# Carried turns sent from SyncE's queue, and the two functions of the sign made on ScalarE for the first group too

## The chip, the core and the metric

The kernel runs on one core of one Trainium2 chip. The metric is the device time of one launch in microseconds (us); where several launches are given, their median. The core has TensorE (PE in the profile, its weight loads PEld), VectorE (DVE), ScalarE (ACT), GpSimd (POOL) and SyncE (SP, which here only issues transfers). ScalarE can issue transfers from its queue as well.

## What is computed

A gated linear recurrence with complex gates, then a feed-forward layer of three maxed projections. Cut to what matters:

```python
q, k, v, a_re, a_im            # each (4, 8, 768, 48): batch, heads, steps, head_dim, float32
mag = sqrt(a_re**2 + a_im**2); scale = minimum(mag, 0.999) / (mag + 1e-6)
a = (a_re + 1j * a_im) * scale
for t in range(768):
    S = a[:, :, t, :, None] * S + k[:, :, t, :, None] * v[:, :, t, None, :]   # complex state, 48 x 48
    y[:, :, t] = einsum('bhd,bhde->bhe', q[:, :, t], S.real)
x = y.transpose(0, 2, 1, 3).reshape(3072, 384)
h = maximum(maximum(x @ w1, x @ w2), x @ w3)      # 384 -> 768
out = h @ w_out                                   # 768 -> 384
```

The four weights come as 64-bit floats, and the kernel rounds them to 32 bits itself, in twelve blocks.

## The kernel before

**Groups and tiles.** The 768 steps are cut into six stretches of 128; two batches go together. That makes 12 groups (g), each of two tiles x = 2g and 2g + 1 (c = 0, 1), one per batch, with 8 heads x 48 = 384 columns each. Within a tile the recurrence is done as small matmuls on blocks.

**From the gates to the rotated k and q.** `gate_steps` (lines 343 to 393) turns a group's a_re and a_im (`ar`, `ai`) into a log magnitude (`Ln`, line 369) and the tangent of half the angle (`w`, line 381). Line 383 takes the sign of `ar`. Two functions of this sign then go into `ai` and `ar`: (1 - sign)/4 at line 385 or 388, and -sign/pi at line 386 or 389. Groups after the first make them on ScalarE, the first group (g = 0, done in two halves of 128x384) on GpSimd. Line 391 takes the carried turn of the group before off the first row of `ai`, on GpSimd. `turns` (lines 395 to 424) takes the arctangent (ScalarE, another activation table, loaded at line 133), multiplies by `ar` (line 401), adds `ai` (line 402), and sums along the steps by matmuls (`cs`, line 410). ScalarE rounds the sum (`t`, line 413), VectorE takes the fraction (`nf`, line 415), and the last rows of `nf` are transferred into `carry` for the next group: four transfers of 0.8 KB per group (line 424), by ScalarE's queue. `sines` (lines 426 to 435) takes |nf| (`af`, line 430) and sine and cosine (`CS`, four activations by line 112). `products` multiplies k and q by magnitudes (line 475), by `CS` into `uk` and `uq` (line 480), and `uk` by `En` (line 485).

**From there to the output.** `turn` transposes uk and uq on TensorE (`tp`) and ScalarE copies them out (`K` line 497, `Q` line 501). `cut` makes decay factors (`F` on TensorE, `f` on ScalarE, line 112). `prep` multiplies by them on VectorE (line 528: Q, KB, QB, QG). `scores` makes A and B on TensorE, `gather` picks them into `atm` (line 576), `state` updates the state (`dk`, lines 624 to 627), `outputs` makes `y`, copied out as `xT` (line 652). The feed-forward part is `up` (three projections: line 668 copies, line 670 takes the maximum) and `op` (line 678 copies out, line 680 writes).

**Weights.** A block is loaded (line 304), and `weight_round` uses ScalarE (lines 330 and 320) and VectorE (lines 331, 333, 321, 322). All twelve blocks are rounded in about the first 105 us, in between the first two groups.

**Order.** The program is written in one order (a first group by hand, then `weave`, which merges steps by written-down fractions, then `group(g)`), and the framework's scheduler orders each engine's queue from it, except that TensorE's order is fixed by hand up to the second group (line 120), and activations that depend on the table keep their order (line 108). Each engine runs its queue strictly in order. PSUM holds four tiles of two banks for all matmul results, so a matmul can wait for a copy-out of an earlier tile. Transfers take turns over eight completion semaphores, whichever queue issues them, and an issue waits until the transfer before it on its semaphore has landed.

Of the kernel before, what the change touches and what calls it, by code (L numbers as in the profile page):

```python
# [16 lines left out]
AF = mybir.ActivationFunctionType  # L17
OP = mybir.AluOpType
# [33 lines left out]
def kernel(  # L52
# [13 lines left out]
    nc = tc.nc  # L66
# [18 lines left out]
    HC = DM // 2  # L85
# [16 lines left out]
    T = {}  # L102
# [8 lines left out]
    def act(**kw):  # L111
        tab(nc.scalar.activation(**kw))  # L112
# [14 lines left out]
    def banks(nm, n=None):  # L127

        ps = psum.tile([P, 2, 512], FP, tag="ps", name=nm)
        return ps if n is None else ps.rearrange("p a n -> p (a n)")[:, 0:n]  # L130
# [204 lines left out]
    def flat(t):  # L335
        return t.rearrange("p c h d -> p (c h d)")
# [6 lines left out]
    def gate_steps(g, cs):  # L343
        lo, hi = cs[0] * DM, (cs[-1] + 1) * DM

        def part(nm):
            t = T[nm, g]
            return (flat(t) if len(t.shape) == 4 else t)[:, lo:hi]

        def s0():  # L350
            if lo == 0:
                for nm in "Lwe":
                    T[nm, g] = nat1.tile([P, W], FP, tag=nm, name=nm)
                T["Ln", g] = nat2.tile([P, W], FP, tag="Ln", name="Ln")
            L, w, ar, ai = part("L"), part("w"), part("ar"), part("ai")
            nc.scalar.activation(out=w, in_=ar, func=AF.Square)
            nc.scalar.activation(out=L, in_=ai, func=AF.Square)

            nc.vector._custom_dve(dve_ops.TENSOR_ADD_SAT, out=L, in0=L, in1=w, s0=LARGE, s1=SMALL)
            act(out=L, in_=L, func=AF.Ln)  # L360

        def s1():

            L, w, e = part("L"), part("w"), part("e")
            act(out=w, in_=L, func=AF.Exp, scale=0.5)
            act(out=e, in_=L, func=AF.Exp, scale=-0.5)
            act(out=e, in_=e, func=AF.Ln, scale=1e-6, bias=1.0)
            nc.scalar.activation(out=L, in_=L, func=AF.Relu, scale=-0.5, bias=lnmax)
            nc.vector.scalar_tensor_tensor(out=part("Ln"), in0=L, scalar=-LNMAX, in1=e, op0=OP.add, op1=OP.add)  # L369

        def s2():

            L, w, e, ar, ai = part("L"), part("w"), part("e"), part("ar"), part("ai")
            nc.scalar.activation(out=e, in_=ar, func=AF.Abs)
            nc.vector.tensor_tensor(out=w, in0=w, in1=e, op=OP.add)
            act(out=L, in_=w, func=AF.Ln)
            act(out=L, in_=L, func=AF.Exp, scale=-1.0)

            (nc.gpsimd if g > 1 else nc.vector).tensor_tensor(out=ai, in0=ai, in1=L, op=OP.mult)  # L379
            nc.vector.tensor_tensor(out=w, in0=w, in1=L, op=OP.mult)  # L380
            nc.vector.scalar_tensor_tensor(out=w, in0=w, scalar=2.0, in1=ai, op0=OP.subtract, op1=OP.mult)

            nc.scalar.activation(out=ar, in_=ar, func=AF.Sign, bias=tiny)
            if g > 0:
                nc.scalar.activation(out=ai, in_=ar, func=AF.Copy, scale=-0.25, bias=0.25)  # L385
                nc.scalar.activation(out=ar, in_=ar, func=AF.Copy, scale=-1.0 / math.pi)
            else:
                nc.gpsimd.tensor_scalar(out=ai, in0=ar, scalar1=-0.25, scalar2=0.25, op0=OP.mult, op1=OP.add)
                nc.gpsimd.tensor_single_scalar(out=ar, in_=ar, scalar=-1.0 / math.pi, op=OP.mult)
            if g % NS > 0:  # L390
                nc.gpsimd.tensor_tensor(out=ai[0:1], in0=ai[0:1], in1=T["carry", g], op=OP.subtract)  # L391

        return [s0, s1, s2]

    def turns(g, cs, meanwhile):

        w, ar, ai = T["w", g], flat(T["ar", g]), flat(T["ai", g])
        for part in [[c] for c in cs] if g == 0 else [cs]:
            n = slice(part[0] * DM, (part[-1] + 1) * DM)
            act(out=w[:, n], in_=w[:, n], func=AF.Arctan)  # L400
            nc.vector.tensor_tensor(out=w[:, n], in0=w[:, n], in1=ar[:, n], op=OP.mult)
            nc.vector.tensor_tensor(out=w[:, n], in0=w[:, n], in1=ai[:, n], op=OP.add)  # L402
        meanwhile(2)
        for c in cs:
            ps = banks("cs", DM)

            for ch in range(2):
                for j in range(2):
                    at = c * DM + j * HC
                    mm(out=ps[j * L64:(j + 1) * L64, ch * HC:(ch + 1) * HC], lhsT=upto[:, ch * L64:(ch + 1) * L64],  # L410
                       rhs=w[:, at:at + HC], start=True, stop=True)
            t = nat2.tile([P, DM], FP, tag="t", name="t")
            nc.scalar.activation(out=t, in_=ps, func=AF.Copy, bias=MAGIC)
            nf = nat2.tile([P, DM], FP, tag="nf", name="nf")
            nc.vector.scalar_tensor_tensor(out=nf, in0=t, scalar=MAGIC, in1=ps, op0=OP.subtract, op1=OP.subtract)
            T["nf", g * C + c] = nf
            if g == 0:
                sines(g, [c])
            if (g + 1) % NS > 0:
                if c == 0:  # L420
                    T["carry", g + 1] = nat1.tile([1, W], FP, tag="carry", name="carry")
                for j in range(2):
                    last, at = (j + 1) * L64, c * DM + j * HC
                    nc.scalar.dma_start(out=T["carry", g + 1][:, at:at + HC], in_=nf[last - 1:last, HC:])

    def sines(g, cs):
        for c in cs:
            nf = T["nf", g * C + c]
            t = nat2.tile([P, DM], FP, tag="t", name="af")
            nc.scalar.activation(out=t, in_=nf, func=AF.Abs)  # L430
            CS = nat2.tile([P, H, 2, D], FP, tag="CS", name="CS")

            act(out=CS[:, :, 0], in_=hv(t), func=AF.Sin, scale=TWOPI, bias=hpi)
            act(out=CS[:, :, 1], in_=hv(nf), func=AF.Sin, scale=-TWOPI)
            T["CS", g * C + c] = CS

    def angles(g, cs, meanwhile=lambda n: None):

        table("trig_and_small")
        turns(g, cs, meanwhile)  # L440
        if g > 0:
            sines(g, cs)
        table("natural_log_exp_and_others")
# [434 lines left out]
```

## Time and profile before

| what | value |
|---|---|
| median of 10 launches | 679.93 us (678.76 to 681.74) |
| the profiled launch, its own time | 680.61 us |
| its span in the profile | 678.9 us |
| busy: PE, DVE, ACT, POOL | 604.5, 496.9, 388.3, 121.3 us |
| mean granted TensorE clock | 0.977 |
| carry transfers from ScalarE's queue | 40 issues, median 0.60 us each, 3.7 us from issue to landing |
| POOL, lines 388 and 389 | 2 + 2 instructions of 128x384: 1.04 and 0.51 us, 1.29 and 1.17 us |
| ACT, lines 385 and 386 (later groups) | 11 + 11 instructions of 128x768, 0.84 us each |

Times are read from one profiled launch, in microseconds from the start of its span. A bracket at the end of a timeline row tells how long the engine stood idle before the row and what ended that; "ACTq" or "SPq" rows are the queue's issue of transfers, which does not count as busy. Rows of a few instructions are merged (x4).

### The profile page before, as it was taken

How to read it: one execution, taken by the hardware profiler on the slowest of the kernel's cores; microseconds unless marked ns; L12 is line 12 of the kernel's file. 1: busy time of each engine (PE TensorE's matmuls, PEld its weight loads, DVE VectorE, ACT ScalarE, POOL GpSimd, SP SyncE). 2: the span in 40 equal slices, each digit the busy share in tenths (PEclk: the TensorE clock that was granted, in tenths of full speed). 3: DMA queues.
4: the chain of work that ended last, by engine and by line, in shares of the span. 5: the costliest groups of instructions: out<-in, count | busy, mean ns of one | idle time of the engine just before them, and what ended most of it. 6: DMA issues, size and time to landing. Idle time of an engine off the chain costs nothing.

```text
span 678.9 us, 24518 instructions
## 1 busy us (share of the span) xinstructions
PE 604.5 (89%) x10844; PEld 497.4 (73%) x10844; DVE 496.9 (73%) x662; ACT 388.3 (57%) x618; POOL 121.3 (18%) x130
## 2 busy tenths in 40 slices
PE   1134677889999999999999999999999999999997
PEld 0033665777878878878878878878878878887785
DVE  4798989986887887887786787788787878755111
ACT  6687776686386386557475565755754854430000
POOL 8500101403213113013013013023023023000000
PEclk9977987999999999999999999999999999999999
DMA  6684443331331331330330331320420220000000
GB/s 134 167 250 96 125 105 65 68 65 35 58 57 33 62 61 25 66 62 19 66 66 16 73 59 27 70 62 18 73 56 15 37 49 2 2 26 3 13 13 24
DMA packets 139050, 39.38 MB, mean 58 GB/s; under 512 B 131648, under 2 KB 134720, under 8 KB 138944
## 3 DMA queue, kind: packets, MB, share of 16 engines
q1 hardware_dynamic: 137664, 37.78, 25.7%
q8 instruction: 85, 1.39, 0.8%
q10 hardware_dynamic: 1280, 0.03, 0.1%
q14 instruction: 21, 0.17, 0.1%
HBM read 33.03 MB, written 4.72 MB: 56 GB/s over the span
## 4 chain that ended last, share of the span: by engine, by line
PE 66%; ACT 12%; DVE 9%; issue 7%; POOL 4%; DMA 1%; ACTq 0%; DVEq 0%; POOLq 0%
PE up L117 33%; PE op L117 13%; PE y L117 6%; PE tp L117 4%; PE B L117 3%; PE cs L117 2%; PE A L117 2%; ACT CS L112 2%; PE dk L117 2%; PE sums L117 1%; ACT e L112 1%; ACT K L497 1%; ACT L133 1%; DVE QB L528 1%; ACT f L112 1%
## 5 line engine op out<-in xcount | busy, mean ns | idle before, releaser
L117 PE MATMUL up<-xT,w 128*128 128x256 f32 (+1 forms) x1404 | 294.5, 367 | 5.2 <-ACT f L112 2.4
L117 PEld LDWEIGHTS up<-xT,w 128*128 128x128 f32 x1404 | 247.8, 191 | 41.9 <-ACT f L112 5.7
L117 PE MATMUL op<-wo,hT 128*128 128x384 f32 x288 | 99.1, 495 | 0.8 <-ACT K L497 0.4
L668 ACT COPY hT<-up 128x768 f32<-128x768 f32 (+2 forms) x27 | 19.6, 725 | 115.2 <-PE up L117 115.2
L117 PEld LDWEIGHTS op<-wo,hT 128*128 128x128 f32 x288 | 53.4, 191 | 35.4 <-ACT K L497 1.4
L670 DVE TENSOR_TENSOR hT<-hT,up 128x768 f32<-128x768 f32 (+2 forms) x54 | 46.3, 857 | 43.5 <-PE up L117 43.0
L379 POOL TENSOR_TENSOR ai<-ai,L 128x768 f32<-128x768 f32 x10 | 21.7, 2174 | 287.3 <-ACT L L112 138.7
L528 DVE TENSOR_TENSOR Q<-Q,f 112x512 f32<-112x512 f32 x48 | 40.5, 844 | 38.3 <-ACT f L112 38.3
L528 DVE TENSOR_TENSOR QB<-Q,f 112x512 f32<-112x512 f32 (+1 forms) x48 | 61.9, 1326 | 0.0
L117 PE MATMUL y<-atm,vb 128*32 128x64 f32 x1536 | 45.8, 227 | 3.1 <-DVE atm L576 2.9
L117 PEld LDWEIGHTS y<-atm,vb 128*32 128x32 f32 x1536 | 39.1, 114 | 12.6 <-issue 8.7
L117 PE MATMUL y<-QG,g 112*32 112x64 f32 x1408 | 44.5, 222 | 0.0
L112 ACT ACTIVATE f<-F 48x296 f32<-48x296 f32 x96 | 39.6, 413 | 0.8
L117 PEld LDWEIGHTS y<-QG,g 112*32 112x32 f32 x1408 | 38.1, 112 | 0.0
L475 POOL TENSOR_TENSOR k<-E,k 128x384 f32<-128x384 f32 x20 | 24.6, 1230 | 69.7 <-ACT E L112 69.7
L117 PE MATMUL B<-QB,KB 112*32 112x80 f32 x1536 | 33.8, 242 | 2.4 <-DVE QB L528 1.9
L485 DVE TENSOR_TENSOR uk<-uk,En 128x768 f32<-128x768 f32 x24 | 22.9, 954 | 17.4 <-PE tp L117 17.4
L117 PE MATMUL sums<-Ln,mid 64*64 64x192 f32 x192 | 14.9, 361 | 22.5 <-DVE Ln L369 22.5
L117 PE MATMUL cs<-w,upto 128*64 128x192 f32 x192 | 19.6, 349 | 17.3 <-DVE w L402 13.8
L391 POOL TENSOR_TENSOR ai<-ai,carry 1x768 f32<-1x768 f32 x10 | 19.2, 1918 | 84.8 <-ACT ai L385 81.4
L117 PE MATMUL tp<-ident,uk 128*112 128x128 f32 x192 | 27.6, 292 | 7.3 <-DVE uk L480 7.3
L576 DVE COPY_PREDICATED atm<-masko,B 128x256 f32<-128x256 uint8 x72 | 31.6, 439 | 3.2
(106 smaller groups left out, 997.9 us busy)
## 6 DMA issues: line engine op xcount, KB each, us to landing
ar<-in_a_re_dram SPq DMA_DIRECT2D x24, 192.0 KB, 3.9
ai<-in_a_im_dram SPq DMA_DIRECT2D x24, 192.0 KB, 3.6
k<-in_k_dram SPq DMA_DIRECT2D x96, 48.0 KB, 2.4
q<-in_q_dram SPq DMA_DIRECT2D x96, 48.0 KB, 2.4
vb<-in_v_dram SPq DMA_DIRECT2D x192, 24.0 KB, 2.2
out_dram<-ot SPq DMA_DIRECT2D x24, 192.0 KB, 2.2
raw<-in_moe_w_dram SPq DMA_DIRECT2D x5, 768.0 KB, 4.9
w<-in_moe_w_dram SPq DMA_DIRECT2D x2, 768.0 KB, 7.0
```

The source lines that it names most:

```text
L112: tab(nc.scalar.activation(**kw))
L117: ins = f(**kw)
L133: tab(nc.scalar.preload_act_table_set(nm))
L379: (nc.gpsimd if g > 1 else nc.vector).tensor_tensor(out=ai, in0=ai, in1=L, op=OP.mult)
L391: nc.gpsimd.tensor_tensor(out=ai[0:1], in0=ai[0:1], in1=T["carry", g], op=OP.subtract)
L475: eng.tensor_tensor(out=hd(T[nm, x]), in0=E, in1=hd(T[nm, x]), op=OP.mult)
L485: nc.vector.tensor_tensor(out=u, in0=u, in1=two(T["En", x]), op=OP.mult)
L497: nc.scalar.copy(out=T["K", x][0:DD], in_=src)
L528: nc.vector.tensor_tensor(out=out, in0=in_, in1=f.to_broadcast([DD, 2 * H - g, n, 8]), op=OP.mult)
L576: nc.vector.copy_predicated(out=out, mask=mask, data=data)
L668: nc.scalar.copy(out=dst, in_=ps)
L670: nc.vector.tensor_tensor(out=dst, in0=dst, in1=ps, op=OP.max)
```

## The change

For the first group the two functions of the sign are made by ScalarE like in all others, and the four carry transfers of each group are issued from SyncE's queue.

```diff
             nc.scalar.activation(out=ar, in_=ar, func=AF.Sign, bias=tiny)
-            if g > 0:
-                nc.scalar.activation(out=ai, in_=ar, func=AF.Copy, scale=-0.25, bias=0.25)
-                nc.scalar.activation(out=ar, in_=ar, func=AF.Copy, scale=-1.0 / math.pi)
-            else:
-                nc.gpsimd.tensor_scalar(out=ai, in0=ar, scalar1=-0.25, scalar2=0.25, op0=OP.mult, op1=OP.add)
-                nc.gpsimd.tensor_single_scalar(out=ar, in_=ar, scalar=-1.0 / math.pi, op=OP.mult)
+            nc.scalar.activation(out=ai, in_=ar, func=AF.Copy, scale=-0.25, bias=0.25)
+            nc.scalar.activation(out=ar, in_=ar, func=AF.Copy, scale=-1.0 / math.pi)
             if g % NS > 0:
                 nc.gpsimd.tensor_tensor(out=ai[0:1], in0=ai[0:1], in1=T["carry", g], op=OP.subtract)
...
-                    nc.scalar.dma_start(out=T["carry", g + 1][:, at:at + HC], in_=nf[last - 1:last, HC:])
+                    nc.sync.dma_start(out=T["carry", g + 1][:, at:at + HC], in_=nf[last - 1:last, HC:])
```

The scheduler orders the queues anew for the changed program. As built, TensorE's queue is the same. Around the change the others differ like this:

- ScalarE, first group: one Copy of each half's pair stands after each of the activations that follow it; the second half's pair lies between the last activations before the first table load. Further on, the second half's `t`, `af`, `CS` and the table load back now stand ahead of the first `K`; before they stood behind it.
- ScalarE, second group: `t`, `t`, one weight step (line 330), `af`, `af`, `CS`; the four carry issues between are gone. Later `K`, `Q`, `f` stand ahead of line 357 where line 357 stood ahead of `K`.
- VectorE: in the first group the first `k` product (line 475) stands ahead of line 381; in the second group the four line 480 products stand ahead of the weight steps of lines 321, 331 and 322, which stood ahead of them; in later groups they alternate with the three `atm` picks from B, which stood ahead of them.
- SyncE: the four carries stand right behind a group's loads of `ar` and `ai` and ahead of its loads of k and q. In the second group they stand between the first `ar` load and the other three of these loads, and the loads of v into the first buffer, which stood ahead of the k and q loads, stand behind them, with the two `ai` loads of the group after behind that.

## The prediction

> **What bounds the kernel now.** I read first the busy time of the engines by stage (columns: stretch, its length, busy time and instructions of PE, PEld, DVE, ACT and POOL, granted clock, share of the transfer engines, GB/s).
>
> ```profile
> 0.00:30.00 30.00, 3.16 (x34) 1.72 (x34) 16.25 (x42) 20.24 (x37) 25.09 (x70) 1.00 0.60 143
> 30.00:50.00 20.00, 8.52 (x141) 7.00 (x145) 18.65 (x27) 15.54 (x24) 0.00 (x0) 0.80 0.86 248
> 50.00:85.00 35.00, 20.59 (x376) 18.27 (x370) 32.37 (x50) 26.14 (x39) 2.04 (x1) 0.82 0.47 111
> 85.00:105.00 20.00, 13.33 (x320) 12.27 (x320) 17.96 (x30) 13.25 (x22) 0.00 (x0) 0.87 0.44 99
> 105.00:133.00 28.00, 23.02 (x548) 19.45 (x540) 26.85 (x31) 19.46 (x30) 9.85 (x6) 0.91 0.30 58
> 133.00:180.00 47.00, 43.49 (x917) 36.89 (x918) 38.11 (x52) 29.61 (x47) 10.29 (x6) 1.00 0.27 51
> 180.00:660.00 480.00, 477.49 (x8483) 391.31 (x8482) 344.84 (x435) 262.95 (x418) 73.99 (x47) 1.00 0.21 41
> ```
>
> From 180 us on TensorE is the bound: it is idle for 480.00 - 477.49 = 2.51 us of 480. Nothing that ScalarE, GpSimd or SyncE saves there is worth more than these 2.5 us, though eight of the ten carries lie there. Before that VectorE is the bound from 30 to 133 us (busy 93, 92, 90 and 96% of the four stretches), because it rounds the weights as well. So the change is worth what it takes out of the first 180 us, as far as VectorE's idle time lets it. Next I read the timelines of VectorE, GpSimd, ScalarE and TensorE there, at the two places that the change touches.
>
> ```profile
> 25.95 0.56 DVE L401 TENSOR_TENSOR w<-w,ar 128x384 f32<-128x384 f32 x1 [1.28 <-POOL maskf L144]
> 28.88 0.56 DVE L401 TENSOR_TENSOR w<-w,ar 128x384 f32<-128x384 f32 x1 [2.37 <-POOL ar L389]
> ...
> 27.08 0.51 POOL L388 TENSOR_SCALAR ai<-ar 128x384 f32<-128x384 f32 x1
> 27.67 1.17 POOL L389 TENSOR_SCALAR ar<-ar 128x384 f32<-128x384 f32 x1
> ...
> 23.02 1.00 ACT L112 ACTIVATE E<-sums 128x384 f32<-128x384 f32 x2 [2.36 <-DVE k L475]
> 24.03 1.28 ACT L133 ACT_TABLE_LOAD   x1
> 37.55 1.01 ACT L497 COPY K<-tp 112x1024 f32<-112x1024 f32 x1 [1.95 <-PE tp L117]
> 86.87 3.70 ACTq L424 DMA_DIRECT2D carry<-nf  x4
> 90.62 0.94 ACT L430 ACTIVATE af<-nf 128x384 f32<-128x384 f32 x2 [3.83 <-DVE ex L331]
> 93.61 1.93 PE L117 MATMUL tp<-ident,uk 128*112 128x128 f32 x8 [3.75 <-DVE uk L480]
> 104.29 0.66 PE L117 MATMUL y<-atm,vb 128*32 128x64 f32 x16 [2.92 <-DVE atm L576]
> ```
>
> Both edits are on the path there. GpSimd gets to the second half's sign functions at 27.08, after its masks, and VectorE stands still 2.37 us for them. ScalarE issues four carries for 3.70 us between `t` and `af`, with `nf` long done (VectorE's L415 pair ran from 86.26 to 87.38), and TensorE waits 3.75 us for what comes of `af`.
>
> **Part 1, the sign functions (0 to 30 us).** GpSimd loses 1.04 + 0.51 + 1.29 + 1.17 = 4.0 us. ScalarE gains four Copies of 128x384; no such row exists, the nearest is L374 of that form: 515 ns long, with the next one starting 0.41 to 0.42 us after it. So 4 x 0.42 = 1.7 us. The first pair falls into ScalarE's 2.36 us of idle time before 23.02. The second pair lies around the last E's, ahead of the table load. In the new order VectorE makes the first k product one instruction (L381, 0.6 us) earlier, and the GpSimd instructions that stretched its neighbours are gone (L379 0.85 against 0.56 in the first half): it starts at about 21.4, not 22.40. Then E at 21.9, Copy 22.5, E 22.95, Copy 23.35, table load 23.75 (before 24.03), arctangent 25.05, and line 401 runs at 25.7 and 26.15 instead of 25.95 and 28.88: 2.7 us won. If k comes no earlier, the second pair sets the table load back by 0.84 us to 24.87 and 1.6 us are won. I take 2.7.
>
> Here a rule of the Trainium skill speaks against the change: "ScalarE: Activation LUTs", in Rules for kernel authors, wants plain multiplies and adds on VectorE, not ScalarE, and budgets about 0.3 us + 0.83 ns per element for an activation. By it each Copy takes 0.3 + 384 x 0.00083 = 0.62 us (an estimate), the second pair costs 0.4 us more than above, and 2.3 us are won. The measured 0.42 us decides; VectorE, which the rule prefers, is the engine that waits.
>
> **Part 2, 30 to 85 us.** The first group's two carries a half are cheap on ScalarE (0.50 to 0.61 us each, mostly beside running activations), but the new order moves the second half's `t`, `af`, `CS` and the 1.28 us table load ahead of K, into the 1.95 us that ScalarE waited at 37.55. Replayed with the durations of the rows: nf at 29.4, uk (L480) at 32.1 (before 34.49), table load done at 35.2, transpose 33.1 to 35.05, K 35.2, the weight steps L330 and L320 0.8 each, Q 37.7, and the four f done at 40.25 where they ended at 45.5: 5.2 us earlier. VectorE cannot follow all of that; in its new order QB ends at 45.0 instead of 49.37, **4.4 us won**. Bounds: 2.7 if VectorE only shifts, 5.2 if it follows. The loads don't stop this: the raw weights were issued at 29.96 to 31.6 and landed 4.8 us later, and the first is wanted at 36.1. From 50 to 85 us VectorE is full in both (one wait of 1.67 us for L330 comes back as about 1.5), so 4.4 us arrive at the next `cs`, at 80.3 instead of 84.74.
>
> **Part 3, the carries of the second group (85 to 105 us).** On the new clock `t` ends at 82.3, L330 (0.8) stands before af at 83.1, the first CS pair is done at 84.85, and L480 starts at 84.9 where it started at 92.50. TensorE's tp comes 7.6 us earlier. But the weight steps that VectorE did meanwhile (0.87 + 0.47 + 0.87 = 2.2 us) now follow, and only VectorE's idle time can be won: 20.00 - 17.96 = 2.0 us, of which one new wait for L320 behind K, Q and two f gives back about 1. So y, after the last atm pick, gains 4.4 + 2.0 - 1.0 = 5.4. **I carry 5.5 us on.**
>
> Here a second rule: "DMA: Bandwidth & Descriptors", section Issuing engines are not separate DMA queues, says that issuing from several engines saves only the sequencer's time to initiate a transfer, usually small relative to the transfer. By it part 3 would be nothing and 4.4 us would be carried on. The row shows 3.70 us of issue in front of af, as long as a carry's 3.7 us to landing; so I keep the 1 us.
>
> **Part 4, 105 to 180 us.** To 133 us VectorE idles 1.15 us of 28: 0 more. K no longer stands behind L357 (0.85 us), which may take 0.4 us off TensorE's wait for f at 123.3; I take 0. From 133 to 180 TensorE idles 47.00 - 43.49 = 3.5 us (0.76 for uk, 0.94 for hT, 0.56 for K, 0.56 for f, the rest smaller). ScalarE gets 2.65 us back in front of af at 138.40, which serves all of these, but K now stands behind two more activations. I take 1.5 of 0 to 3.
>
> **Part 5, SyncE and the rest.** SyncE issues 40 x 0.60 = 24 us more. In a steady group it is free from 184.56 to 189.74, between its last `ai` issue and its first k load, and four carries take 2.4 us; nf is done at 184.0 and the k loads behind wait for uk later anyway. In the first group its loads stood still 6.0 us until 38.52 for a carry of ScalarE's on their semaphore; that goes. The carry is read (L391) a group later. VectorE's atm picks, now alternating with L480, end some 2.5 us later (190.2 for 187.7 at the steady group of 183 us), and y needs them at about 198. After 180 us I count 0 (bounds 0 and 1.5).
>
> **Sum.** 5.5 + 1.5 = 7.0 us, from the profiled launch's own 680.61: 673.6. The median of the runs lies 0.7 below that launch, so 679.93 - 7.0 = **672.9 us**.
>
> **Rivals.** *Half of it.* VectorE is at 90 to 96%: what TensorE and ScalarE win early is only work put off, part 2 keeps 2.7 and part 3 gives 1: 3.7, and little after; 676.2. For it: the full row of VectorE. Against: in part 2 it has 1.35 us idle plus a shorter stretch to fill.
>
> *Slower.* The loads of v that now stand ahead of the `ai` loads of g = 3. On the old clock k and q are issued until 106.8; two blocks of v follow, at 5.95 us each as at 107.49, or 9.26 as at 85.36; then the `ai` loads land (2.9 us) at about 123, at worst 129. ScalarE reaches L357 at 123.2. If they land later than that, ScalarE stands, and behind it are En, E, the table load and the arctangent, then L401 and cs on the path; it turns into a loss once it exceeds the 5.5 us, at about 128.7. With v, k and q all at the slower rate (12 us of k and q become 18), landing at 135 costs 11.8 - 5.5 = 6.3: 686. Against: k and q start 7 us earlier with uk.
>
> *No change.* Both edits only fill waits, VectorE is saturated from the first weight on, and the order costs as much as it gains: 679.9. Against: 2.37 us idle at 28.88 on the bounding engine.
>
> **Chances.** The forecast 0.62 (its own range 669.5 to 675.5), half 0.22, no change 0.05, slower 0.11. A difference of 0.2%, 1.36 us, is about the least that can be told from none. Faster: 0.62 + 0.22 = 0.84; within: 0.05; slower: 0.11. The range runs from 669.0, where the upper bounds of parts 2 and 4 and of the rest (0.8 + 1.5 + 1.5) are all but reached, to 677.5, which takes in the half case: 0.16 is left out above.
>
> **What would show it.** Right: line 401's second row near 26.2 with no GpSimd wait; QB done near 45; no ACTq rows, af within 1 us of `t` and L330; TensorE's wait at the second tp below 1 us; TensorE idle some 2.5 us of the last 480 before the tail. Wrong: a wait of ScalarE for `ai` at L357 near 117, SyncE still in v loads there, or VectorE waits for L330 or L320 of several us between 50 and 100.

## The result, and the profile after

Fourteen launches of the changed kernel have a median of 676.11 us (673.23 to 678.15), beside 679.58 us for 49 launches of the kernel before. The ratio is 0.9945, 95% interval 0.9932 to 0.9958: 3.7 us won (2.9 to 4.6), where 7.0 were forecast. The profiled launch took 676.42 us, its span is 674.7 us, its mean granted clock 0.972. From line 390 of before on, line numbers are four lower (397 is the arctangent's product, 411 `nf`, 471 the k product, 476 `uk`, 497 `Q`, 572 `atm`, 622 the state).

Busy time by stage, with the columns of the first view of the prediction:

```profile
0.00:30.00 30.00, 5.95 (x48) 3.40 (x48) 18.89 (x48) 22.93 (x44) 23.11 (x66) 1.00 0.60 144
30.00:50.00 20.00, 9.75 (x183) 8.65 (x184) 19.49 (x29) 14.61 (x22) 0.00 (x0) 0.73 0.90 255
50.00:85.00 35.00, 21.56 (x378) 18.55 (x381) 30.17 (x45) 26.31 (x40) 2.04 (x1) 0.74 0.45 122
133.00:180.00 47.00, 44.69 (x921) 37.48 (x915) 37.12 (x49) 29.89 (x49) 9.72 (x6) 1.00 0.23 43
180.00:660.00 480.00, 477.07 (x8389) 391.38 (x8378) 339.75 (x433) 261.49 (x414) 73.53 (x47) 1.00 0.20 41
```

GpSimd's four instructions at the start are gone, but its busy time fell only from 25.09 to 23.11 us, since its masks took 2.0 us longer. Behind 180 us TensorE idles 2.93 us, before 2.51: hardly anything changed there. But VectorE, which should have become fuller from 50 to 85 us, is emptier (30.17 against 32.37), and the clock is lower in two stages (0.73 for 0.80 and 0.74 for 0.82). Now the rows that answer to those shown of before (start, duration, engine, line, operation):

```profile
24.88 1.15 DVE L397 TENSOR_TENSOR w<-w,ar 128x384 f32<-128x384 f32 x2 [1.67 <-ACT w L112]
...
34.89 1.01 ACT L493 COPY K<-tp 112x1024 f32<-112x1024 f32 x1
...
54.06 0.56 DVE L331 TENSOR_SCALAR ex<-ex 128x768 f32<-128x768 f32 x1 [2.32 <-ACT ex L330]
57.28 0.96 DVE L321 CUSTOM_DVE_ANT_0 ex<-w,ex 128x1536 uint16<-128x1536 uint16 x1 [0.98 <-ACT w L320]
...
81.15 2.83 PE L117 MATMUL cs<-w,upto 128*64 128x192 f32 x16 [3.43 <-DVE w L398]
...
85.21 0.93 ACT L426 ACTIVATE af<-nf 128x384 f32<-128x384 f32 x2
...
88.87 1.08 PE L117 MATMUL tp<-ident,uk 128*112 128x128 f32 x8
...
100.45 0.57 PE L117 MATMUL y<-atm,vb 128*32 128x64 f32 x16 [4.50 <-DVE atm L572]
```

Of the kernel before, `cs` was not shown yet:

```profile
84.74 1.52 PE L117 MATMUL cs<-w,upto 128*64 128x192 f32 x16 [3.43 <-ACT ex L330]
```

Every wait that the change was to remove is gone: VectorE's 2.37 us for GpSimd, ScalarE's 1.95 us before K, its four carry issues before `af`, TensorE's 3.75 us before the second `tp`. Yet others have grown: VectorE's waits for L330 and L320, and TensorE's wait for the last pick before y (4.50 us for 2.92). And `cs` itself takes 2.83 us where it took 1.52.

When comparing the two launches a start-up difference has to come off. The first half's `Ln` (L369) ran at 12.20 us here and at 13.11 us before, ahead of everything that the change touches. The column of these two launches in the table has this 0.9 us taken off; that is the most it can be worth, since in a kernel whose GpSimd makes the sign functions an early start was partly lost (`e_carry`, below).

| gain at | forecast | changed against before, less 0.9 | the same pair with TensorE kept busy (below) |
|---|---|---|---|
| end of the arctangent's products | 2.7 | 2.5 | 2.7 |
| end of QB | 4.4 | 3.7 | 4.0 |
| second group's `cs` | 4.4 | 2.7 | 3.1 |
| `uk`, second group | 7.6 | 4.5 | 6.0 |
| y behind the last pick | 5.4 | 2.9 | 6.1 |
| `cs` of g = 2 | 5.5 | 2.2 | 5.5 |
| `cs` of g = 3 | 7.0 | 3.2 | 6.6 |
| span | 7.0 | 3.3 | 5.8 |

### The profile page after: what moved, and what is told of

Read it like the earlier page. It is cut to its first block, busy times and chain, and to the rows that moved or that the text cites. A ratio compares the mean times of both kernels' runs of the same rounds, so it can differ in the third digit from the quotient of the medians.

```text
span 674.7 us, 24524 instructions
## 1 busy us (share of the span) xinstructions
PE 607.2 (90%) x10844; PEld 498.7 (74%) x10844; DVE 490.0 (73%) x662; ACT 390.4 (58%) x622; POOL 119.1 (18%) x126
## 4 chain that ended last, share of the span: by engine, by line
PE 59%; ACT 14%; issue 5%; DVE 2%; DMA 0%; POOL 0%; POOLq 0%; ACTq 0%; DVEq 0%
PE up L117 29%; PE op L117 13%; PE y L117 6%; PE tp L117 2%; ACT CS L112 2%; ACT e L112 2%; PE B L117 2%; PE cs L117 2%; PE sums L117 2%; ACT L133 2%; PE dk L117 1%; PE A L117 1%; ACT K L493 1%; DVE Ln L369 1%; ACT ar L383 1%
## 5 line engine op out<-in xcount | busy, mean ns | idle before, releaser
L524 DVE TENSOR_TENSOR QB<-Q,f 112x512 f32<-112x512 f32 (+1 forms) x48 | 53.3, 1148 | 0.0
L117 PEld LDWEIGHTS y<-atm,vb 128*32 128x32 f32 x1536 | 39.2, 114 | 13.9 <-issue 10.6
L524 DVE TENSOR_TENSOR KB<-K,f 112x768 f32<-112x768 f32 x24 | 38.2, 1590 | 0.0
L357 ACT ACTIVATE L<-ai 128x768 f32<-128x768 f32 (+1 forms) x13 | 10.3, 793 | 40.0 <-DVE w L380 32.6
```

Source lines behind the costliest of these rows:

```text
L117: ins = f(**kw)
L524: nc.vector.tensor_tensor(out=out, in0=in_, in1=f.to_broadcast([DD, 2 * H - g, n, 8]), op=OP.mult)
```

## The experiments

**My theory** after the comparison: part 1 is right; part 2's new order gave nothing that lasted; parts 3 and 4 are worth 1 to 2 us, of which TensorE's half clock at `cs` hid some. Rivals: the sign edit is the whole gain; the new order is the whole gain; the half clock only covers waits for a full VectorE. Ratios below are to the kernel before on the same chip, with their 95% intervals; 0.001 is 0.68 us.

### Each edit alone

`e_sign` has only the first hunk of the diff, `e_carry` only the second.

> Only the sign edit; the carries stay on ScalarE's queue. As built, ScalarE's queue keeps the second half's af, CS and the table load behind the first K, so this run has part 1 without parts 2 and 3. Theory (the two edits add up, the sign edit gives the 2.6 us seen at the arctangent's product): 677.0, line 397's second row near 25.4, K near 35, but f still done some 8 us behind K as before. Rival A (the sign edit is the whole gain, the carries are worth nothing): 675.9, as fast as the changed kernel. Rival B (VectorE is full, an earlier start is only put off, and the new order is the whole gain): 679.4.

Measured 676.91 us, ratio 0.9955 (0.9936 to 0.9975). The product's rows run from 25.00 to 26.03, K at 34.15, f ends 8.0 us behind it. The theory's number; 675.9 lies in the interval too.

> Only the carry edit; the first group's two functions of the sign stay on GpSimd. As built, ScalarE's second half (t, af, CS, table load) stands ahead of the first K here too. Theory (edits add up): 678.2, about 1.3 us below the kernel before, line 401's second row still near 28.9, f done 1.5 to 2.5 us earlier than 45.5. Rival A (carries worth nothing): 679.6. Rival B (the order is the whole gain): 676.2.

Measured 678.61 us, 0.9985 (0.9966 to 1.0004); line 401's second row at 28.08, f done at 44.0 instead of 45.5 (0.8 us of that was there at line 401 already, in a launch that began 1.9 us earlier). The theory's number again, though a carry edit worth nothing lies in the interval too. 3.1 and 1.0 us add up to 4.1, the measured gain of both is 3.7. That the new order is the whole gain is out.

### Part 2 taken apart from parts 3 and 4

`carry_first` sends only the first group's carries from SyncE, `carry_later` only those of later groups; both have the sign edit.

```diff
-                    nc.sync.dma_start(out=T["carry", g + 1][:, at:at + HC], in_=nf[last - 1:last, HC:])
+                    (nc.sync if g == 0 else nc.scalar).dma_start(out=T["carry", g + 1][:, at:at + HC], in_=nf[last - 1:last, HC:])
```

> Both edits, but only the first group's carries go through SyncE's queue, those of all later groups stay on ScalarE's. As built, the queues are those of the changed kernel up to the second group's t, so this is part 2 without parts 3 and 4. Theory (part 2's new order is given back as waits of VectorE for the weight steps of ScalarE that now stand behind K, Q and f, before the next cs): 676.9, as the sign edit alone. Rival (part 2 is worth its 1.7 us and parts 3 and 4 nothing): 675.5 to 676.1.

Measured 678.40 us, 0.9974 (0.9958 to 0.9989): against the sign edit alone 1.3 us slower (± 1.7). The rival's gain is out. The two profiles start alike (first `Ln` at 12.37 and 12.41), so they can be laid side by side. VectorE's rows, first of the sign edit alone:

```profile
44.30 1.82 DVE L524 TENSOR_TENSOR QB<-Q,f 112x512 f32<-112x512 f32 x2
59.60 0.96 DVE L369 SCALAR_TENSOR_TENSOR Ln<-L,e 128x768 f32<-128x768 f32 x1 [0.41 <-ACT L L368]
```

and of the same kernel with part 2:

```profile
43.00 1.82 DVE L524 TENSOR_TENSOR QB<-Q,f 112x512 f32<-112x512 f32 x2
59.46 0.96 DVE L369 SCALAR_TENSOR_TENSOR Ln<-L,e 128x768 f32<-128x768 f32 x1
```

QB is 1.3 us earlier, as forecast nearly (1.7); 16 us later `Ln` is 0.14 us earlier, and the next `cs` 0.25 us later (79.80 for 79.55). VectorE's waits from 30 to 80 us say why (us in total, number, longest), first of the sign edit alone:

```profile
DVE uk L476 <- ACT CS L112: 0.7, 1, 0.7
DVE g L622 <- ACT g L620: 0.5, 1, 0.5
DVE Ln L369 <- ACT L L368: 0.4, 1, 0.4
DVE ex L331 <- ACT ex L330: 0.4, 1, 0.4
```

and with part 2:

```profile
DVE ex L331 <- ACT ex L330: 1.0, 1, 1.0
DVE ex L321 <- ACT w L320: 1.0, 1, 1.0
DVE Q L524 <- ACT f L112: 0.4, 1, 0.4
DVE w L375 <- ACT e L374: 0.3, 1, 0.3
```

That is 2.0 us in four waits and 2.7 us in four others. The new order took away the wait for CS and put weight steps of ScalarE (L330, L320) behind K, Q and f, where VectorE then met them too early. But order is not all that differs in these two launches. K waits for the transposes `tp` on TensorE, and these ran at another clock, first in the sign edit alone:

```profile
48.56 1.45 PE L117 MATMUL tp<-ident,uk 128*112 128x128 f32 x8
49.85 1.04 PE L117 MATMUL tp<-ident,uq 128*112 128x128 f32 x8
```

and with part 2:

```profile
47.25 1.96 PE L117 MATMUL tp<-ident,uk 128*112 128x128 f32 x8
49.00 1.79 PE L117 MATMUL tp<-ident,uq 128*112 128x128 f32 x8
```

Together they took 1.3 us longer, which is more than the wait for L330 (1.0). So the profiles alone cannot say how much of what came back is the order and how much the clock; the times of the runs say that nothing of QB's 1.3 us was left.

> Both edits, but the first group's carries stay on ScalarE's queue and all later ones go through SyncE's: the sign edit with parts 3 and 4, without part 2. As built, the queues are those of the sign edit alone up to the second group's t, and close to those of the changed kernel behind it. Theory (part 2 is worth nothing, since VectorE is full there and each wait it loses comes back before the next cs): as fast as the changed kernel or up to 1.3 us faster, 674.8 to 676.1. Rival (part 2 is worth the 1.7 us that QB's time showed): 677.8.

Measured 676.89 us, 0.9950 (0.9929 to 0.9971). By the ratio as fast as the changed kernel (0.9945), so leaving part 2 out costs 0.3 us (± 1.7); the bare time lies between the two expectations, but the kernel before, measured beside it, ran 0.6 us slower as well (680.22). Together the two runs put part 2 at nothing, not at 1.7. Parts 3 and 4 are worth the rest: the changed kernel is 2.0 us (± 1.4) below `carry_first`; 2.6 were forecast.

### TensorE's clock

The granted clock in the profiles is 1.00 or 0.50 and changes at times a multiple of some 3.41 us apart; in the changed kernel at 39.2, 52.8, 56.3, 66.5, 80.1, 86.9, 100.5, 104.0, 107.5 and 110.9. Three such windows around its second group's `cs`, with the stage columns:

```profile
76.76:80.17 3.41, 0.96 (x9) 0.77 (x7) 3.41 (x7) 0.97 (x2) 0.00 (x0) 0.99 0.00 0
80.17:83.58 3.41, 2.43 (x16) 1.90 (x16) 2.90 (x4) 0.49 (x1) 0.00 (x0) 0.50 0.60 198
83.58:86.99 3.41, 3.41 (x76) 2.97 (x73) 2.69 (x6) 2.98 (x7) 0.00 (x0) 0.51 0.40 96
```

and of the kernel before:

```profile
79.45:82.86 3.41, 1.86 (x17) 1.67 (x15) 3.41 (x8) 1.88 (x3) 0.00 (x0) 1.00 0.09 17
82.86:86.27 3.41, 1.53 (x22) 1.28 (x26) 3.41 (x5) 1.40 (x2) 0.00 (x0) 1.00 0.83 192
```

TensorE stood idle for the same 3.43 us ahead of `cs` in both. Here 0.96 us of work fell into one window, and the next two ran at half clock, with cs, A and a part of `up` in them; before, the idle time was cut in two by the window's edge (1.86 and 1.53 us of work), and the clock stayed. The Trainium skill, "TensorE: Matmul & The Clock Gate", Part 1: The HAM clock gate, states the rule: the clock is halved after an idle window of 3.4 us, on windows that run freely and do not start with the kernel. The trace agrees on length and halving; what it adds is that a window with 28% of work was idle enough.

To take the clock out, matmuls that nobody reads were put into idle TensorE, into a PSUM tile which the next real matmuls overwrite. In these kernels the queues of VectorE, ScalarE and SyncE are tied to the order that they had without the fill.

```diff
             ps = banks("cs", DM)
+            [mm(out=ps[:, 0:P], lhsT=upto, rhs=ident, start=True, stop=True) for _ in range(20 if g == 1 and c == 0 else 0)]
...
         ps = banks(nm)
+        [mm(out=ps[:, 0, 0:P], lhsT=upto, rhs=ident, start=True, stop=True) for _ in range(36 if x == 0 and nm == "A" else 0)]
```

> The changed kernel with every queue in its own order, and 20 matmuls of 128x128 more on TensorE ahead of the second group's first cs, into the same PSUM tile, which cs overwrites: they fill 2.5 us of the 3.43 us that TensorE stood idle there. Theory (in the changed kernel the half clock that follows this idle time took 1.3 us of what part 3 should have won): granted clock 1.00 from 78 to 88 us, cs 1.5 us long for 2.83, and 674.9, 1.2 us below the changed kernel. Rival (VectorE is the bound there and TensorE's clock is only cover): 676.1, as the changed kernel.

Measured 674.44 us, 0.9913 (0.9893 to 0.9934), 2.2 us (± 1.7) below the changed kernel; clock 1.00 from 74 to 88 us, cs 1.52 us. This is the theory's side.

> As the run before, and 36 such matmuls ahead of the first A, where TensorE stood idle for 5.80 us (4.5 us of it filled). Theory (the half clock also sets the time from QB to the second tile's K, and so VectorE's wait of 2.32 us for L330): clock 1.00 from 39 to 53 us, A 0.9 us for 1.51, B 1.3 for 2.35, tp 1.1 for 1.96, K some 2 us earlier, VectorE's wait for L330 near 54 gone, and 673.0. Rival (VectorE only puts its work off, the waits come back behind): 675 to 676.

Measured 673.72 us, 0.9907 (0.9885 to 0.9928), the fastest of all: 2.6 us (± 1.7) below the changed kernel. TensorE's rows:

```profile
37.28 8.30 PE L117 MATMUL A<-ident,upto 128*128 128x128 f32 x72
45.51 0.89 PE L117 MATMUL A<-Q,K 112*32 112x48 f32 x64
46.22 1.30 PE L117 MATMUL B<-QB,KB 112*32 112x80 f32 x64
47.45 1.09 PE L117 MATMUL tp<-ident,uk 128*112 128x128 f32 x8
...
75.31 4.63 PE L117 MATMUL cs<-ident,upto 128*128 128x128 f32 x40
79.87 1.52 PE L117 MATMUL cs<-w,upto 128*64 128x192 f32 x16
```

VectorE's waits from 30 to 80 us, which were 2.3, 1.0, 0.3 and 0.3 us in the changed kernel:

```profile
DVE ex L321 <- ACT w L320: 0.4, 1, 0.4
DVE Q L524 <- ACT f L112: 0.4, 1, 0.4
DVE w L375 <- ACT e L374: 0.3, 1, 0.3
```

A, B and tp take what was expected at full clock, K runs at 48.58 instead of 50.46, and in the same order the wait for L330 is gone. So this wait hung on the half clock as well as on the order. The fill came out twice as long as meant, since each of these matmuls is two rows of 0.115 us: it held A and cs back, cs by 1.1 us behind VectorE's L398 (done at 78.75). The time fell all the same, so the rival, that TensorE's clock is only cover, is out.

> The kernel before with every queue in its own order and the same fill: 36 matmuls of 128x128 ahead of the first A and 20 ahead of the second group's first cs. Theory (half clock after idle time costs both kernels alike, so it is no reason for the shortfall): 677.2, about 2.4 us below the kernel before, and 3.5 us above the changed kernel with both fills (673.7). Rival (in the profile the half clock fell on cs in the changed kernel only, so it ate what part 3 should have won): 679.0, hardly below the kernel before, and 5.3 us above the changed kernel with fill.

Measured 679.14 us, 0.9969 (0.9950 to 0.9988), beside 680.2 for the kernel before. The fill is worth 2.1 us (± 1.3) before and 2.6 us (± 1.7) after by the ratios, which is the theory; the bare times (679.14 and 673.72, 5.4 us apart) are the rival's. The intervals leave it open. The profiles speak for the rival. These two start alike (first `Ln` at 13.07 and 13.11) and give the table's last column: the forecast's 5.4 and 5.5 at y and the next `cs` are there, though with other shares (3.1 for 4.4 at `cs`), so that they meet is in part luck. In the kernel before with fill TensorE still waited for `uk`, behind the carries:

```profile
91.58 1.93 PE L117 MATMUL tp<-ident,uk 128*112 128x128 f32 x8 [3.54 <-DVE uk L480]
```

so its earlier `cs` (1.8 us ahead of the kernel before without fill) had shrunk to 0.3 us at the `cs` of g = 2. The changed kernel has no such wait and kept its gain.

> Only the sign edit, its queues in their own order, with both fills. It shows what the carry edit is worth once TensorE's clock is out of it (against 673.7 with both edits and both fills). Theory (the carry edit's 1 us comes from the stretch behind 130 us, where TensorE waits for ScalarE, and is there at full clock too): 674.6. Rival A (at full clock parts 2 and 3 come out as forecast): 676.5 or more. Rival B (the carry edit is worth nothing): 673.7.

Measured 674.91 us, 0.9922 (0.9899 to 0.9944). The theory's number; 673.7 lies in the interval too (`fill_both` is 1.0 us faster, ± 2.1), 676.5 does not.

> Only the carry edit, in its own order, with both fills: the fourth corner beside neither edit (679.1), the sign edit (674.9) and both edits (673.7) at full clock. Theory (the edits add up): 677.9. Rival (without the sign edit the carry edit is worth its forecast, and they overlap): 675.5.

Measured 675.84 us, 0.9932 (0.9910 to 0.9953): the theory's 677.9 is missed, the rival's 675.5 met. With the fill the sign edit wins 3.2 us, the carry edit 2.5, both together 4.2 (each ± 2.0). Alone they seem to overlap, since either one makes the first group's second half earlier and VectorE can use that once; the intervals don't prove it.

> The same kernel in its own order with both fills (36 matmuls ahead of the first A, 20 ahead of the second group's first cs). Theory: as the changed kernel with both fills or faster, 673.0 to 673.7. Rival (part 2 is worth something at full clock): 675.4.

Measured 675.18 us, 0.9921 (0.9894 to 0.9949): between the two, and against `fill_both` (1.0 us slower, ± 2.4) it decides nothing. The two profiles start alike (first `Ln` at 13.22, in `fill_both` 13.11): `Ln` near 59 us runs at the same time with and without part 2 (58.57 and 58.60), the `cs` of g = 2 is 0.8 us earlier with it (127.23 for 128.03). So a part of part 2 may be there with the fill.

```diff
+        [mm(out=y[:, 0], lhsT=upto, rhs=ident, start=True, stop=True) for _ in range(28 if x == 2 else 0)]
```

> As the run before, with 28 such matmuls more ahead of the second group's first y, where TensorE stood idle for some 5 us and then ran A, B and op at half clock from 101 to 108. Theory (VectorE, busy over 95% there, sets the time): clock 1.00 from 92 to 110, but no more than 0.5 us won, 672.7. Rival (TensorE's half clock is on the path here as well): 671.0.

Measured 680.16 us, 0.9988 (0.9971 to 1.0006), 5.0 us slower than without. A miss of mine: the y behind the idle time at 92 to 97 us is that of tile 1, and the fill went to tile 2:

```profile
118.75 3.90 PE L117 MATMUL up<-xT,w 128*128 128x128 f32 x18 [1.43 <-ACT f L112]
122.49 6.42 PE L117 MATMUL y<-ident,upto 128*128 128x128 f32 x56
```

It tells something else: 6.42 us of useless work at 122 us made the next cs 7.0 us later (135.00 for 128.03). From some 120 us on TensorE's queue is on the path, though VectorE is busier in that stage. Whether the half clock at 95 to 109 us costs anything was not tried.

### Where a carry stands on ScalarE

`carry_late` is the changed kernel with the carries on ScalarE's queue again, each group's four tied in right behind the table load that follows CS.

> The changed kernel with its queues in their order, but the carries are issued from ScalarE's queue again, in each group right behind the activation table load that follows CS. Theory (what the carries cost is only that af and CS stood behind them): 676.3, as the changed kernel, with ScalarE's issue time, some 2.4 to 3.7 us a group, in front of K at no price beyond a few tenths. Rival (the issue time on ScalarE is what costs, wherever it stands, since K, Q and f stand behind it): 678 or more, with TensorE waiting 2 us or more longer for f and K around 95 and 145 us.

Measured 697.07 us, 1.0254 (1.0228 to 1.0280). The rival's direction, far beyond its number. Up to the `cs` of g = 2 it is as fast as the changed kernel (129.15 us for 129.91). Then each later group that sends carries loses; TensorE's waits from 180 to 660 us:

```profile
PE dk L117 <- DVE hT L666: 7.7, 7, 1.3
PE op L117 <- ACT K L493: 5.6, 7, 1.2
```

and ScalarE at the first of these groups:

```profile
183.63 1.28 ACT L133 ACT_TABLE_LOAD   x1
184.67 2.06 ACTq L420 DMA_DIRECT2D carry<-nf  x2
186.78 0.84 ACT L112 ACTIVATE L<-L 128x768 f32<-128x768 f32 x1 [1.86 <-DVE atm L572]
...
193.68 0.99 ACT L493 COPY K<-tp 112x1024 f32<-112x1024 f32 x1
```

In the changed kernel this L starts right behind the table load (183.97), and K 6.9 us later, as here. So 1.9 us in front of a chain of seven activations to K cost TensorE 1.9 us (13.3 / 7) in each of seven groups, where 3.39 us in front of `af` at 183.37 had cost the kernel before next to none. But only half of the 1.9 us is the length of the issues, which take 0.51 us each. The profile's chain of what released what (start, duration) shows the rest:

```profile
183.94 2.26 DMA k<-in_k_dram
186.20 0.02 issue
186.22 0.51 ACTq L420
186.73 0.05 issue
186.78 0.85 ACT L L112
```

The last carry's issue stood until a k load of SyncE had landed, and ScalarE's queue with it. The same pair, a k load landed and then this issue, stands in front of L in six of the seven groups. Some 5 us of the rest are TensorE's own: it is busy 612.6 us for 607.2, at a clock of 0.98 in the stretches with these waits. What stands behind an issue, and what it has to wait for itself, matter more than its length.

## Why the forecast had the right sign and twice the size

**Part 1 held.** The products end 2.5 to 2.7 us earlier (forecast 2.7), and the sign edit alone is worth 3.1 us (1.7 to 4.4). The Copies run in front of the table load as replayed (it starts at 23.03, with the start's 0.9 us 23.9, for 23.75). Each was 0.51 to 0.52 us long, and the next activation began 0.42 to 0.47 us after it did (0.42 were counted); the 0.62 us that part 1 set against this rest on a budget that the Trainium skill ("ScalarE: Activation LUTs", Rules for kernel authors) gives for an activation whose bias is a pointer operand, and these Copies have a constant.

**Part 2 failed: "in its new order QB ends at 45.0 instead of 49.37".** QB ended at 44.85, with the start's 0.9 us 45.8, so the time itself nearly came. But a time on a full engine isn't a gain: VectorE reached QB earlier by leaving weight steps for later. The 1.7 us beyond part 1 were not there (-1.3 and +0.3 us, ± 1.7 each). The words "one wait of 1.67 us for L330 comes back as about 1.5" sized this wrongly: it came back as 2.32, with 0.98 for L320 and 0.30 for L374 beside it. What could be won was VectorE's idle time, and the new order exchanged it for other waits. How long these are hangs on TensorE's clock too (with the fill the one for L330 is gone); how the loss divides between order and clock is not shown.

**Part 3 was right in kind.** The issues in front of `af` are gone, and so is TensorE's wait for `tp`. At the unlucky clock of the profiled launch y gained no more than cs; with the fill it gained 3.1 us more (6.1 for 3.1, forecast 1.1). Of this the sign edit alone has 1.7 (`sign_fill`, from 3.3 at cs to 5.0 at y, with 1.5 us of start taken off), which leaves some 1.3 for the carries. The rule of "DMA: Bandwidth & Descriptors" that I set aside for the 3.70 us row does not fit here: four issues of 0.8 KB hold the queue as long as one takes to land (3.7 us), and `carry_late` shows that the queue's time at these issues, put in the wrong place, costs up to 21 us.

**The clock was left out.** My replay gave cs 1.5 us, the row of before, which lay in a fully clocked window by chance. In the changed kernel cs, A and `up` took 2.83, 1.51 and 2.35 us for 1.52, 0.89 and 1.60. No term of the forecast stood for that. How much of the missing 3.3 us this is in the median stays open: 0.5 us by the ratios of the filled and unfilled pairs (4.2 against 3.7), some 2 by their bare times and profiles. Part 2's 1.7 and this are about the gap.

**Part 4** (1.5): from the `cs` of g = 2 to that of g = 3, 1.1 us unfilled and 1.1 filled. TensorE's idle time in the stage fell from 3.5 to 2.3 us. **Part 5** (0): after 180 us little moved (TensorE idles 0.4 us more; with the fill 0.8 us of 6.6 were lost). Seven of the ten groups of carries lie there, not eight as the forecast has it, which changes nothing. The *slower* rival did not come: the `ai` loads of g = 3 were issued at 111.99, and L357 ran at 119.73 with no wait. The *half* rival gave 676.2 for the same reason as part 2's failure, a full VectorE; its time was right, and it is half of the cause. The forecast's own range, 669.5 to 675.5, just missed 676.11.

## What to carry to other kernels

Where one engine is full over a stretch, forecast from the sum of its idle time there, not from when one of its results arrives: an earlier result may only have changed places with work that comes due later, so follow the wait list to the end of the stretch. Before using a matmul's duration at a new time, look at which clock window it fell into. An issue on a compute engine's queue is priced by what stands behind it and by the landing that it waits for itself, so move it behind the chain that feeds the bounding engine, or to a queue with nothing behind it.

## What the hardware showed that I had not expected

- An idle gap of one length (3.43 us) halved TensorE's clock in one launch and not in another, by where 3.41 us windows fell: after windows with 0.96 us and 0.16 us of work (28 and 5%) it was halved, after 1.53 and 1.86 us (45 and 54%) not. The rule isn't complete: ahead of the first halving, in the changed kernel at 39.2 us, windows with less work left the clock at 1.00 (0.37 us from 29.0 to 32.4 us, 11%).
- The first `Ln` differs by 2.0 us between the profiled launches (11.25 to 13.22 us). With GpSimd making the sign functions an early start was lost: in `e_carry`, at 11.25, VectorE waited 3.63 us for `ar`.
- A transfer's issue on ScalarE's queue waited for a load that SyncE had issued: in `carry_late` it began 0.02 us after the k load had landed (186.22 and 186.20), and the activations behind it stood still meanwhile.
- Keeping TensorE busy with work that nobody reads won 2.6 us (± 1.7), though the fill was twice as long as meant.
